# Attention and gated MLP in one kernel: 12 transposes per head, seven PSUM banks for the last batch, and an order written by the kernel's own list scheduler

## The chip, the cores and the metric

The kernel runs on one core of a Trainium2 chip. The time is the device time of one execution in microseconds (us). Of the kernel before there are three runs: 828.46, 829.50 and 830.23 us, median 829.5 us. The engines are called PE (TensorE), PEld (its weight load), DVE (VectorE), ACT (ScalarE), POOL (GpSimd) and SP (SyncE, which issues all of this kernel's DMAs).

## The reference, cut to what matters

```python
# attention: q, k, v are (8, 8, 576, 64), s is (8, 8, 576)
scores = q @ k.T / 8
cum    = cumsum(max(s, 0))
scores = where(causal, scores + min(-(cum_q - cum_k), 0), -1e9)
attn   = exp(scores - max) ; attn /= sum(attn) + 1e-9
x      = (attn @ v) with the 8 heads of a batch side by side       # (8, 576, 512)
# MLP, for each of the 8 batches
h      = gelu_tanh(x @ w_in)                                        # (576, 1024)
u, v   = h[:, :512], h[:, 512:]
v_n    = layer norm of v over its columns * g_ln
v_s    = w_sg @ v_n + b_sg                                          # over the 576 tokens
out    = x + (u * v_s) @ w_out
```

## The kernel before, in words

There are 64 heads, and after every eighth a batch of the MLP has its input. Heads 0 to 11 run attention in fp32; from head 12 on (scores from head 8) each operand is split in two fp32r parts, high and low, and a product is two or three matmuls into one PSUM bank.

One head, in the code's steps:

- `load(h)` (L102) issues the DMAs of k, q and v; for heads 0 to 7 the row of running sums `cf` follows into `kf` (L109). `split_head(h)` (L272) splits k and q on ACT and POOL and moves the parts with five DMAs (L281 to L285).
- `scores(h)` computes five blocks of queries (`it` 0 to 4, with 64, 128, 128, 128, 128 rows and 64, 192, 320, 448, 576 keys). Each goes from PSUM through DVE (L305, mask and running minimum) into a buffer `p` (`pbuf[h % 2][it]`), and ACT takes the exponential in place (L315).
- `norm` (L318) divides by the row sums, mostly on POOL (L338). Blocks that do not fill 128 rows or columns are copied into spare columns of others at that step: block 0 goes into columns 384 to 447 of block 3.
- `transposes(h)` puts 128x128 pieces of the normed blocks through PE (L377) into four PSUM tiles `pt`, 13 transposes per head; one of them, `tr(t, 0, 4, 512, 64)`, is the last corner of block 4 (keys 512 to 575) and fills only 64 rows. ACT and DVE copy each tile to SBUF (`pa`, `pb`, `pd`).
- `pv(h)` multiplies them with v into `xx` and `x0` (L450, L468 to L472), and ACT and DVE write the result into `xr`.

One batch of the MLP, `ffn(b)`: POOL splits `xr` into `xs` (L90, L93). Then units, each of which fills one PSUM bank: 5 `v` units (matmul `vm`, L510 to L527; the last reads its small operand `xq` by DMA, L520), 8 `u` units (`um`, L574), 8 `s` units (`sm`, L589 to L593) and 8 `o` units (`om`, L608). After `vm` and `um` the bank is held until DVE, ACT and POOL are through with the gelu (L493 to L496, L539 to L548).

PSUM has eight banks: two for `sc`, two for `pt`/`x0`, one for `xx`, three for all MLP units (`ps_m`).

What sets the order: every step is placed at a time in units of heads (`place`, `spread`), and the program is recorded in that order. The tile framework's scheduler then orders the instructions of each engine by its own cost model; the recorded order is its priority. All engines run their own queue strictly in order.

Of the kernel before, what the change touches and what calls it, by code (L numbers as in the profile page):

```python
# [8 lines left out]
F32 = mybir.dt.float32  # L9
# [40 lines left out]
ENG = {'k': 'sg', 'vs': 'sg', 'xs': 'gg', 'ln': 'sg', 'gt': 'sg', 'w': 'gg', 'ws': 'sv', 'n': 'ggggg', 'n0': 'gggsg', 'ws1': 'g'}  # L50
MT = 52.0
F6 = [2.0, 9.4]
F7 = [2.0, 9.4]
F0 = [1.9, 9.6]
POS = dict(load=-1.8, split=-0.18, sc=(0, 0, 0, 0), tr=(0, 0, 0, 0), pv=(0, 0.1, 0.1), wv=(0.1, 6.0),
           wu=(7.0, 10.0), ws=(9.0, 11.0), wo=(11.0, 14.0), f0=2.0, f1=9.6)


@with_exitstack
def tile_attn_gmlp(  # L60
# [11 lines left out]
):  # L72
    nc = tc.nc

    const = ctx.enter_context(tc.tile_pool(name="const", bufs=1))
    att = ctx.enter_context(tc.tile_pool(name="att", bufs=2))
    moe = ctx.enter_context(tc.tile_pool(name="moe", bufs=1))
    ps_sc = ctx.enter_context(tc.tile_pool(name="ps_sc", bufs=2, space=bass.MemoryType.PSUM))
    ps_pt = ctx.enter_context(tc.tile_pool(name="ps_pt", bufs=2, space=bass.MemoryType.PSUM))
    ps_x = ctx.enter_context(tc.tile_pool(name="ps_x", bufs=1, space=bass.MemoryType.PSUM))  # L80
    ps_m = ctx.enter_context(tc.tile_pool(name="ps_m", bufs=3, space=bass.MemoryType.PSUM))

# [14 lines left out]
    first = []  # L97

    def later():
        return tc.issue_after(first[0].ins)  # L100

# [22 lines left out]

    dram = ctx.enter_context(tc.tile_pool(name="dram", bufs=1, space=bass.MemoryType.DRAM))
    cum = dram.tile([2, BH, S], F32, name="cum")
# [191 lines left out]
    def norm(h, its, rs):  # L318
# [52 lines left out]
    def transposes(h):  # L371
# [42 lines left out]
        t = ps_pt.tile([P, 512], F32, name="pt", tag="pt")  # L414
        tr(t, 0, 4, 512, 64)
        tr(t, 64, 3, 384)
        tr(t, 192, 4, 384)
        if h < NP:
            pt["pd"] = (att.tile([P, 320], F32, name="pdh", tag="pdh", bufs=1),)
            nc.vector.tensor_copy(out=pt["pd"][0][0:64, 0:64], in_=t[0:64, 0:64])  # L420
# [11 lines left out]
    def pv(h):  # L432
# [34 lines left out]
        if f32:  # L467
            nc.tensor.matmul(xx[0:rows, 256:320], st(4)[0:REM], pd[0][0:REM, 0:64], start=False, stop=True)  # L468
            nc.tensor.matmul(x0[0:rows, 0:64], st(0), pd[0][:, 64:128], start=True, stop=True)
        else:  # L470
# [13 lines left out]
    def ffn(b):  # L484
        xs = []
        for c in range(NC):
            t = moe.tile([P, 2, S], F32R, name="xs", tag="xs", bufs=4)
# [80 lines left out]
        def u_unit(ch, dt):  # L568
            cs = slice(ch * CH, ch * CH + CH)
            ps = ps_m.tile([P, 512], F32, name="um", tag="m")  # L570
            n = 0
# [10 lines left out]
        def s_unit(ch, dt):  # L582
            cs = slice(ch * CH, ch * CH + CH)
            ds_ = slice(dt * P, (dt + 1) * P)
            ps = ps_m.tile([P, 512], F32, name="sm", tag="m")
            n = 0
# [14 lines left out]
        def o_unit(ch, mt):  # L601
            cs = slice(ch * CH, ch * CH + CH)
            ms = slice(mt * P, (mt + 1) * P)
            ps = ps_m.tile([P, 512], F32, name="om", tag="m")
            n = 0
# [35 lines left out]

    def spread(gen, t0, t1, total):
        done = [0.0]

        def go():
            c = next(gen, None)
            if c is not None:
                done[0] += c
# [68 lines left out]
```

## Time and profile before

| | |
|---|---|
| median of three runs | 829.5 us |
| the profiled execution's own time | 829.98 us |
| its span, first to last instruction | 828.2 us |
| mean granted clock of PE | 0.992 |
| busy: PE, PEld, DVE, ACT, POOL | 794.3, 695.6, 597.6, 577.4, 597.6 us |

The span is 1.8 us shorter than the execution's own time. A busy PE in this profile means that some matmul is under way; matmuls overlap, so the time that one costs is the distance to the start of the next, not its own length.

### The profile page before, as it was taken

The numbers are of one execution on the slowest core, as the hardware profiler recorded it, in microseconds if no ns is written. First come the engines' busy times: TensorE is split into PE (matmuls) and PEld (weight loads), VectorE is DVE, ScalarE is ACT, GpSimd is POOL, SyncE is SP. The second block draws the span as 40 slices with busy tenths as digits, with TensorE's granted clock in tenths as the row PEclk, the third lists the DMA queues.
The fourth block names the chain that finished last, engine by engine and source line by source line (L and its number), as shares of the span: only waits on it lengthen the run. The fifth ranks groups of instructions, "written<-read, shape, count | busy, mean of one in ns | idle before, by whom it ended". The sixth has DMA issues, their size and how long they took to land.

```text
span 828.2 us, 16736 instructions
## 1 busy us (share of the span) xinstructions
PE 794.3 (96%) x5161; PEld 695.6 (84%) x5161; DVE 597.6 (72%) x1806; ACT 577.4 (70%) x1620; POOL 597.6 (72%) x979
## 2 busy tenths in 40 slices
PE   6899999899999999999999999999999999998898
PEld 3455666799989998999989997899989998997798
DVE  5995468975787678966887687965897678963552
ACT  4787778875686678867787677866887678853340
POOL 4987668888677767796778777796778778782541
PEclk9999999999999999999999999999999999999999
DMA  7656553334342453444434443444434443300001
GB/s 218 193 171 183 146 136 87 95 98 115 104 106 71 128 131 86 103 122 127 118 85 105 130 132 73 113 121 109 112 101 112 122 127 87 99 25 30 27 7 58
DMA packets 69804, 89.29 MB, mean 108 GB/s; under 512 B 25954, under 2 KB 42212, under 8 KB 69716
## 3 DMA queue, kind: packets, MB, share of 16 engines
q1 hardware_dynamic: 69716, 88.23, 40.6%
q8 instruction: 41, 0.67, 0.4%
q14 instruction: 47, 0.39, 0.2%
HBM read 42.27 MB, written 9.73 MB: 63 GB/s over the span
## 4 chain that ended last, share of the span: by engine, by line
PE 73%; DVE 13%; DMA 6%; ACT 3%; issue 3%; POOL 2%; SPq 1%; DVEq 0%; POOLq 0%; ACTq 0%
PE om L608 12%; PE sm L589 11%; PE um L574 10%; PE vm L510 9%; PE xx L450 9%; PE pt L377 8%; PE sc L297 4%; PE sc L298 4%; DVE p L305 2%; DMA q<-k 2%; PE sm L593 1%; DMA xq<-xs 1%; PE sm L592 1%; DVE vm L496 1%; DVE wbits L220 1%
## 5 line engine op out<-in xcount | busy, mean ns | idle before, releaser
L338 POOL TENSOR_SCALAR p<-p,rs 128x448 f32<-128x448 f32 (+4 forms) x372 | 181.0, 500 | 30.5 <-DVE rs L321 10.9
L315 ACT ACTIVATE p<-p,mn 128x448 f32<-128x448 f32 (+4 forms) x320 | 177.9, 557 | 25.5 <-DVE mn L305 23.4
L305 DVE CUSTOM_DVE_ANT_0 p<-sc,mask 64x64 f32<-64x64 f32 (+4 forms) x320 | 126.2, 422 | 55.3 <-PE pt L377 29.6
L377 PE MATMUL pt<-ident,p 128*128 128x128 f32 (+1 forms) x832 | 136.6, 278 | 4.6 <-DVE pbl L389 2.6
L574 PE MATMUL um<-xs,wi 128*128 128x288 f32 x768 | 124.1, 303 | 4.0 <-DVE vt L548 2.0
L589 PE MATMUL sm<-ws,vn 128*128 128x288 f32 x768 | 127.1, 300 | 0.4 <-DVE u L496 0.4
L93 POOL TENSOR_TENSOR k<-raw,k 128x576 fp32r<-128x576 f32 x56 | 80.6, 1439 | 63.7 <-ACT k L88 34.1
L608 PE MATMUL om<-gt,wo 128*128 128x288 f32 x768 | 125.6, 299 | 0.0
L574 PEld LDWEIGHTS um<-xs,wi 128*128 128x128 f32 x768 | 110.0, 191 | 10.3 <-DVE u L496 3.2
L377 PEld LDWEIGHTS pt<-ident,p 128*128 128x128 f32 (+1 forms) x832 | 97.0, 138 | 20.6 <-DVE pbl L389 5.4
L608 PEld LDWEIGHTS om<-gt,wo 128*128 128x128 f32 x768 | 110.5, 188 | 2.6 <-DVE ot L612 0.3
L589 PEld LDWEIGHTS sm<-ws,vn 128*128 128x128 f32 x768 | 109.9, 189 | 2.6 <-DVE u L496 1.5
L510 PE MATMUL vm<-wi,xs 128*128 128x512 f32 x384 | 105.5, 407 | 4.4 <-DVE u L496 2.2
L297 PE MATMUL sc<-k,q 128*128 128x448 f32 x336 | 100.7, 308 | 1.4 <-DVE mn L305 0.8
L298 PE MATMUL sc<-k,q 66*128 66x448 f32 x336 | 89.2, 298 | 0.4 <-DMA k<-cum 0.3
L88 ACT CAST pbh<-pt 128x512 fp32r<-128x512 f32 x104 | 49.0, 479 | 58.1 <-PE pt L377 58.0
L510 PEld LDWEIGHTS vm<-wi,xs 128*128 128x128 f32 x384 | 71.6, 194 | 20.8 <-DVE u L496 2.4
L93 POOL TENSOR_TENSOR gt<-u,gt 128x288 fp32r<-128x288 f32 x64 | 50.9, 807 | 44.3 <-ACT gt L88 43.9
L93 DVE TENSOR_TENSOR pbl<-pt,pbh 128x512 fp32r<-128x512 f32 x104 | 56.6, 549 | 16.8 <-ACT pbh L88 16.7
L297 PEld LDWEIGHTS sc<-k,q 128*128 128x128 f32 x336 | 60.6, 180 | 9.1 <-DVE mn L305 3.6
L298 PEld LDWEIGHTS sc<-k,q 66*128 66x128 f32 x336 | 60.7, 181 | 5.9 <-issue 0.8
L88 ACT CAST k<-raw 128x576 fp32r<-128x576 f32 x56 | 37.6, 671 | 38.8 <-PE sc L297 33.3
(142 smaller groups left out, 1703.2 us busy)
## 6 DMA issues: line engine op xcount, KB each, us to landing
q<-k SPq DMA_DIRECT2D x168, 144.0 KB
raw<-in_kq SPq DMA_DIRECT2D x56, 288.0 KB
vr<-in_vp SPq DMA_DIRECT2D x52, 192.0 KB
out_t<-ot SPq DMA_DIRECT2D x64, 144.0 KB
k<-k SPq DMA_DIRECT2D x56, 144.0 KB
wraw<-in_w_in SPq DMA_DIRECT2D x16, 256.0 KB
kf<-in_kq SPq DMA_DIRECT2D x8, 288.0 KB
qf<-in_kq SPq DMA_DIRECT2D x8, 288.0 KB
```

The lines of the kernel that those rows point to most:

```text
L88: nc.scalar.copy(out=hi, in_=src)
L93: eng_lo.tensor_tensor(out=lo, in0=src, in1=hi.bitcast(F32), op=ALU.subtract)
L297: nc.tensor.matmul(o, d["q1"][:, i0:i0 + r], d["k1"][:, j0:j1], start=True, stop=False)
L298: nc.tensor.matmul(o, q2[h % 2][:, i0:i0 + r], d["k2"][0:66, j0:j1], start=False, stop=True)
L305: nc.vector.tensor_tensor_reduce(out=pbuf[h % 2][it][0:r, j0:j1], in0=pst[0:r, c0:c0 + j1 - j0], in1=(mask2 if it in (2, 4) else mask)[0:r ...
L315: nc.scalar.activation(out=p, in_=p, func=AF.Exp, bias=d["mn"][0:r, it:it + 1], scale=-1.0, accum_out=sums[h % 2][0:r, it:it + 1])
L338: e.tensor_scalar(out=po, in0=pi, scalar1=f, scalar2=1.0, op0=ALU.mult, op1=ALU.mult)
L377: nc.tensor.transpose(out=ps[0:n, c:c + P], in_=pb[it][:, jb:jb + n], identity=ident)
L510: nc.tensor.matmul(ps[0:r], xs[c][:, xi, ts_], wi[:, c, wj, fs], start=(n == 0), stop=(n == 11))
L574: nc.tensor.matmul(ps[:, 0:CH], wi[:, c, wj, dt * P:(dt + 1) * P], xs[c][:, xi, cs], start=(n == 0), stop=(n == 11))
L589: nc.tensor.matmul(ps[:, 0:CH], vn[j][:, vi, ds_], ws[:, j, wj, cs], start=(n == 0), stop=False)
L608: nc.tensor.matmul(ps[:, 0:CH], wo[:, c, wj, ms], gt[ch, c][:, gi, :], start=(n == 0), stop=(n == 11))
```

## The change

It has four parts.

1. `norm` writes the last corner of block 4 into columns 448 to 511 of block 3 (rows 0 to 63), as a separate POOL instruction behind a shorter one for the rest of block 4. The transpose of block 3's last 128 columns then carries the corner along, and the 13th transpose is gone. The evacuation of that tile is cut differently: from head 12 on ACT copies 64x64 and 128x256 instead of 64x128 and 128x192, and DVE has three subtractions (64x64, 64x64, 128x192) instead of two; for heads 0 to 11 one DVE copy goes. In instructions: 64 transposes fewer on PE, 64 more on POOL, 40 more on DVE (104 and 52 fewer, 12 fewer).
2. `ffn` takes its PSUM banks for the last batch in turn from three pools, seven banks in all.
3. All calls are recorded in a `Program` first. `graph` finds their dependencies, `cost` gives each a duration by formula, and `plan` is a list scheduler: of the instructions that are ready it takes the one that can start first, at a tie the one with the lowest key (the step's place in heads). `emit` records them in the order of the planned starts and ties each engine to it. A transfer is planned to move 1300 ns after its issue at the earliest, one transfer after another at 280 GB/s, and its reader to start 600 + 1060 + 100 ns later.
4. Two positions: `split` from -0.18 to -0.4, the end of `wv` from 6.0 to 7.5.

```diff
+LATENCY = [[54, 38, 39, 80, 60], [54, 35, 33, 77, 60], [54, 34, 35, 90, 60], [55, 34, 35, 80, 60], [1060] * 5]
+OVERLAP = [0, 93, 75, 25, 0]
+MARGIN = 100.0
+ISSUE = 450.0
...
+    def cost(self, op):
...
+            if name == "transpose":
+                d, load = 110.0, 56.0
...
+            v = (outs or big)[0]
+            d, load = v.dims[0][1] * v.columns() * 4 / 280.0, ISSUE
...
+def plan(cost, pre, first, uses, order, bufs, prio, after, slack=(0, 0, 0, 0, 0), window=48):
...
+            for c in cand:
+                if c[0] <= least + slack[e]:
+                    if best is None or c[0] < best[0]:
+                        best = (c[0], e, c[1], c[2])
+                    break
...
+        elif e == SP:
+
+            moved = max(moved, s + 1300) + d
+            free[e], end = s + load, moved + 600
...
+            elif it == 4:
+                o = [(p[:, 0:512], p[:, 0:512], rs[:, 4:5]),
+                     (pbuf[h % 2][3][0:64, 448:512], p[0:64, 512:S], rs[0:64, 4:5])]
...
-        tr(t, 0, 4, 512, 64)
         tr(t, 64, 3, 384)
         tr(t, 192, 4, 384)
...
-            nc.scalar.copy(out=hi[0:64, 0:128], in_=t[0:64, 0:128])
-            nc.scalar.copy(out=hi[:, 128:320], in_=t[:, 128:320])
-            nc.vector.tensor_tensor(out=hi[64:128, 0:128], in0=t[0:64, 0:128], in1=hi[0:64, 0:128].bitcast(F32),
+            nc.scalar.copy(out=hi[64:128, 0:64], in_=t[64:128, 64:128])
+            nc.scalar.copy(out=hi[:, 64:320], in_=t[:, 64:320])
+            nc.vector.tensor_tensor(out=hi[0:64, 0:64], in0=t[64:128, 64:128], in1=hi[64:128, 0:64].bitcast(F32),
+                                    op=ALU.subtract)
+            nc.vector.tensor_tensor(out=hi[64:128, 64:128], in0=t[0:64, 64:128], in1=hi[0:64, 64:128].bitcast(F32),
                                     op=ALU.subtract)
...
+        rings = cycle([(ps_m, "m"), (ps_sc, "sc"), (ps_m, "m"), (ps_pt, "pt"), (ps_m, "m"), (ps_sc, "sc"), (ps_pt, "pt")]
+                      if b == B - 1 else [(ps_m, "m")])
...
-            ps = ps_m.tile([P, 512], F32, name="vm", tag="m")
+            ps = bank("vm")
...
+    cost, pre, new, uses, order, bufs, after = nc.graph()
+    prio = [(op["key"], n) for n, op in enumerate(nc.ops)]
+    t, start, _, seqs = plan(cost, pre, new, uses, order, bufs, prio, after)
+    nc.emit(tc, new, uses, seqs, start)
```

Three places of the order matter below. All recorded calls have one line in the changed kernel (L283), so the names tell what a row is.

The first instructions of SP, before: `st` is the input of the running sums, with which everything begins; `kf`, `qf`, `vf` are head 0's and then head 1's.

```order
L128 DMA st<-in_s_t 128x320
L107 DMA kf<-in_kq 128x576
L108 DMA qf<-in_kq 128x576
L118 DMA vf<-in_vp 128x6x64
L107 DMA kf<-in_kq 128x576
```

The same place after the change:

```order
L283 DMA kf<-in_kq 128x576
L283 DMA qf<-in_kq 128x576
L283 DMA vf<-in_vp 128x6x64
L283 DMA st<-in_s_t 128x320
L283 DMA kf<-in_kq 128x576
```

`st` went from first to fourth: head 1's `load` has the key 1 - 1.8 = -0.8, and the start of the program has 0.

PE at the first heads, before, from the first transposes of head 0 on (`p_3_151` is block 3 of head 0, `sc` from `kf` are the scores of head 2):

```order
L377 MATMUL pt<-ident,p_1_148 128x128
L377 MATMUL pt<-ident,p_3_151 128x128 x2
L377 MATMUL pt<-ident,p_4_153 128x128
L295 MATMUL sc<-kf,qf 128x448
L295 MATMUL sc<-kf,qf 64x64
L295 MATMUL sc<-kf,qf 128x320
L295 MATMUL sc<-kf,qf 128x192
L377 MATMUL pt<-ident,p_2_149 128x128
```

After the change, from the end of head 1's product with v on:

```order
L283 MATMUL xx<-pbl,vf 64x448
L283 MATMUL xx<-pbl,vf 64x320
L283 MATMUL xx<-pdh,vf 64x192
L283 MATMUL xx<-pdh,vf 64x64
L283 MATMUL x_377<-pdh,vf 64x64
L283 MATMUL sc<-kf,qf 128x448
L283 MATMUL sc<-kf,qf 64x64
L283 MATMUL sc<-kf,qf 128x320
L283 MATMUL sc<-kf,qf 128x192
L283 MATMUL vm<-wi,xs 128x512
```

The scores of head 2 no longer stand between the transposes of head 0 but behind all work of heads 0 and 1.

PE at the end of the last head, before (`xx` and `x_10809` are its product with v, `vm` and `um` from `xs` are units of the last batch, `om` of the one before):

```order
L608 MATMUL om<-gt,wo 128x288 x12
L450 MATMUL xx<-pdh,vs 128x192
L472 MATMUL x_10809<-pdh,vs 128x64
L450 MATMUL xx<-pdl,vs 128x192
L450 MATMUL xx<-pdh,vs 128x64
L510 MATMUL vm<-wi,xs 128x512 x2
L574 MATMUL um<-xs,wi 128x288
```

After the change (four units of `sm` stand where one and the dots are):

```order
L283 MATMUL xx<-pdh,vs 128x64
L283 MATMUL om<-gt,wo 128x288 x9
L283 MATMUL sm<-ws,vn 128x288 x12
L283 MATMUL sm<-wr_878,vnr_10640 128x288
L283 MATMUL sm<-wr_892,vnr_109 128x288
...
L283 MATMUL om<-gt,wo 128x288 x24
L283 MATMUL vm<-wi,xs 128x512 x6
L283 MATMUL om<-gt,wo 128x288 x12
L283 MATMUL vm<-wi,xs 128x512 x6
```

Between the last matmul of the last head and the first that reads its `xs` there were none; now there are 101 of 288 columns (9 + 56 + 24 + 12) and nine of 512.

## Rows read from the trace of the kernel before

**Rows 1.** The page, parts 1 and 4: busy time, and the chain that ended last.

```profile
PE 794.3 (96%) x5161; PEld 695.6 (84%) x5161; DVE 597.6 (72%) x1806; ACT 577.4 (70%) x1620; POOL 597.6 (72%) x979
PE 73%; DVE 13%; DMA 6%; ACT 3%; issue 3%; POOL 2%; SPq 1%; DVEq 0%; POOLq 0%; ACTq 0%
```

**Rows 2.** Windows: stretch, busy us of PE, PEld, DVE, ACT, POOL; clock, DMA share, GB/s.

```profile
3.00:6.00 3.00, 0.10 (x1) 0.14 (x1) 2.46 (x6) 0.00 (x0) 1.46 (x3) 1.00 0.97 279
...
24.00:41.00 17.00, 15.45 (x62) 7.68 (x60) 15.21 (x43) 12.39 (x37) 15.81 (x25) 0.91 0.58 182
...
60.00:180.00 120.00, 114.47 (x638) 80.81 (x638) 84.50 (x278) 93.69 (x270) 92.24 (x150) 1.00 0.51 130
180.00:740.00 560.00, 553.37 (x3847) 515.80 (x3846) 426.76 (x1305) 419.21 (x1180) 430.48 (x705) 1.00 0.42 106
...
760.80:764.20 3.40, 3.37 (x9) 2.46 (x10) 0.48 (x1) 0.90 (x2) 1.41 (x1) 0.50 0.12 43
```

**Rows 3.** Timeline of PE at the end: start, us, line, count [idle before, releaser].

```profile
756.51 1.74 PE L608 MATMUL om<-gt,wo 128*128 128x288 f32 x12
...
758.40 0.21 PE L450 MATMUL xx<-pdh,vs 128*128 128x64 f32 x1
760.77 1.22 PE L510 MATMUL vm<-wi,xs 128*128 128x512 f32 x2 [2.15 <-POOL xs L90]
...
769.69 2.96 PE L510 MATMUL vm<-wi,xs 128*128 128x512 f32 x12
...
778.06 4.50 PE L510 MATMUL vm<-wi,xs 128*128 128x512 f32 x12 [2.21 <-DVE u L496]
...
787.99 3.19 PE L574 MATMUL um<-xs,wi 128*128 128x288 f32 x12 [2.01 <-DVE vt L548]
```

**Rows 4.** Timeline of all engines behind the last head.

```profile
760.80 1.41 POOL L93 TENSOR_TENSOR xs<-xr,xs 128x576 fp32r<-128x576 f32 x1
```

**Rows 5.** Groups by line and form: busy us, mean ns of one, idle before.

```profile
L377 PE MATMUL pt<-ident,p 128*64 128x128 f32 x64 | 17.6, 276 | 2.1 <-DVE pbl L389 1.8 <-DVE pbl L93 0.3
...
L338 POOL TENSOR_SCALAR p<-p,rs 128x576 f32<-128x576 f32 x64 | 49.1, 767 | 0.0
...
L338 POOL TENSOR_SCALAR p<-p,rs 64x64 f32<-64x64 f32 x128 | 44.2, 346 | 6.1
...
L427 DVE TENSOR_TENSOR pdh<-pt,pdh 64x128 fp32r<-64x128 f32 x52 | 14.8, 284 | 4.4 <-ACT pdh L426 3.0
```

**Rows 6.** Timeline of PE at the first heads.

```profile
25.07 3.15 PE L295 MATMUL sc<-kf,qf 128*128 128x448 f32 x8
...
46.74 0.86 PE L377 MATMUL pt<-ident,p 128*128 128x128 f32 x6
```

**Rows 7.** Timeline of SP at the start.

```profile
0.79 0.39 SPq L128 DMA_DIRECT2D st<-in_s_t  x1
1.23 0.42 SPq L107 DMA_DIRECT2D kf<-in_kq  x1
...
2.89 0.63 SPq L107 DMA_DIRECT2D kf<-in_kq  x1
```

**Rows 8.** Timeline of DVE at the start.

```profile
3.37 0.48 DVE L200 MEMSET vnr<- 2x512 f32 x1
3.89 0.81 DVE L134 TENSOR_SCALAR st<-st 128x320 f32<-128x320 f32 x1
```

**Rows 9.** Waits of PE from 180 to 740 us: total, times, longest.

```profile
PE vm L524 <- DMA xq<-xs: 2.0, 2, 1.4
...
PE sm L593 <- DMA vnr<-vnr: 0.9, 2, 0.4
```

**Rows 10.** The chain around 500 us: start, us from issue to reader.

```profile
502.88 3.65 DMA q<-k
...
507.11 3.36 DMA xq<-xs
```

More of the change, by code (lines that the diff above doesn't have):

```diff
@@ L1 @@
[L1 to L2 removed]
+from bisect import bisect_left, insort
+from contextlib import ExitStack, contextmanager
+from itertools import count, cycle
 import concourse.bass as bass
@@ new lines, with __init__, step, __getitem__ @@
+class View:
+    def __init__(self, buf, dims, off, dt, how):
+        self.buf, self.dims, self.off, self.dtype, self.how = buf, dims, off, dt, how
+    def step(self, dims, off, how, dt=None):
+        return View(self.buf, dims, off, dt or self.dtype, self.how + [how])
+    def __getitem__(self, key):
+        ks = key if isinstance(key, tuple) else (key,)
+        dims, off = [], list(self.off)
+        for n, (s, c) in enumerate(self.dims):
+            k = ks[n] if n < len(ks) else slice(None)
+            a, b = (k, k + 1) if isinstance(k, int) else (k.start or 0, c if k.stop is None else k.stop)
+            off[n == 0] += a * (1 if n == 0 else s)
+            if n == 0 or not isinstance(k, int):
+                dims.append((s, b - a))
+        return self.step(dims, off, lambda x: x[key])
+    def rearrange(self, text, **kw):
+        dims = self.dims
+        if "(" in text:
+            n = 1
+            for _, c in dims[1:]:
+                n *= c
+            dims = [dims[0], (dims[-1][0], n)]
+        return self.step(dims, self.off, lambda x: x.rearrange(text, **kw))
+    def bitcast(self, dt):
+        return self.step(self.dims, self.off, lambda x: x.bitcast(dt), dt)
+    def columns(self):
+        n = 1
+        for _, c in self.dims[1:]:
+            n *= c
+        return n
+    def span(self):
+        lo = self.off[0]
+        return (self.off[1], self.off[1] + self.dims[0][1], lo,
+                lo + 1 + sum(s * (c - 1) for s, c in self.dims[1:]))
+    def make(self):
+        x = self.buf.make()
+        for f in self.how:
+            x = f(x)
+        return x
@@ new lines, in plan, with put, grant @@
+def plan(cost, pre, first, uses, order, bufs, prio, after, slack=(0, 0, 0, 0, 0), window=48):
+    n = len(cost)
+    left = [len(p) for p in pre]
+    succ = [[] for _ in range(n)]
+    for i, p in enumerate(pre):
+        for q in p:
+            succ[q].append(i)
+    issue = [[] for _ in range(n)]
+    for i, qs in after.items():
+        for q in qs:
+            issue[q].append(i)
+            left[i] += 1
+    owner, remain = {}, {}
+    for i in range(n):
+        for b in first[i]:
+            owner[b] = i
+            left[i] += 1
+        for b in uses[i]:
+            remain[b] = remain.get(b, 0) + 1
+    ready = [[] for _ in range(5)]
+    at = [0.0] * n
+    tagof = {b: t for t, bs in order.items() for b in bs}
+    free_slots = {t: [0.0] * bufs[t] for t in order}
+    nxt = {t: 0 for t in order}
+    last = {}
+    def put(j):
+        left[j] -= 1
+        if left[j] == 0:
+            insort(ready[cost[j][0]], (prio[j], j))
+    def grant(t):
+        while free_slots[t] and nxt[t] < len(order[t]):
+            b = order[t][nxt[t]]
+            nxt[t] += 1
+            f = free_slots[t]
+            x = min(f)
+            f.remove(x)
+            j = owner[b]
+            at[j] = max(at[j], x)
+            put(j)
+    for i in range(n):
+        if left[i] == 0:
+            insort(ready[cost[i][0]], (prio[i], i))
+    for t in order:
+        grant(t)
+    free = [0.0] * 5
+    start, fin = [0.0] * n, [0.0] * n
+    pest = peocc = moved = 0.0
+    held = asked = (0.0, 0.0)
+    seqs = [[] for _ in range(5)]
+    for _ in range(n):
+        best = None
+        for e in range(5):
+            cand, least = [], 1e18
+            for pr, i in ready[e][:window]:
+                if e == PE:
+                    s = max(pest + peocc, max(at[i], pest) + cost[i][2])
+                    soon = pest + peocc + 1
+                else:
+                    s = max(at[i], free[e])
+                    soon = free[e]
+                cand.append((s, pr, i))
+                least = min(least, s)
+                if s <= soon:
+                    break
[3 more added lines that the diff above has]
+                        best = (c[0], e, c[1], c[2])
+                    break
+        if best is None:
+            return None
+        s, e, pr, i = best
+        del ready[e][bisect_left(ready[e], (pr, i))]
+        _, d, load, wide, lock = cost[i]
+        if e == PE:
+            pest, peocc, end = s, d, s + d + 60
+            free[e] = s
+        elif e == SP:
+            moved = max(moved, s + 1300) + d
+            free[e], end = s + load, moved + 600
+        else:
+            if e == DVE and wide and held[0] <= s < held[1]:
+                s = held[1]
+            if e == POOL and lock and asked[0] <= s < asked[1]:
+                s = asked[1]
+            end = s + d
+            if wide:
+                asked = (s, end)
+            if lock:
+                held = (s, end)
+            free[e] = end - OVERLAP[e]
+        start[i], fin[i] = s, end
+        seqs[e].append(i)
+        for j in issue[i]:
+            at[j] = max(at[j], s)
+            put(j)
+        for j in succ[i]:
+            ej = cost[j][0]
+            at[j] = max(at[j], s if e == ej == PE else end + LATENCY[e][ej] + MARGIN)
+            put(j)
+        for b in uses[i]:
+            remain[b] -= 1
+            last[b] = max(last.get(b, 0.0), end)
+            if remain[b] == 0:
+                free_slots[tagof[b]].append(last[b] + 60)
+                grant(tagof[b])
+    return max(fin), start, fin, seqs
```

212 lines of the change are left out of this document (187 added, 25 removed).

## The prediction

> **What bounds the kernel now.** I read the page's busy times first, then the chain, then the windows by stage, and only then the timeline where the windows show PE idle. PE is busy in 96% of the span, and its lines hold 73% of the chain that ended last; DVE, ACT and POOL are busy for 70 to 72% each [rows 1]. The windows say where that holds. From 180 to 740 us PE is idle for 6.6 of 560 us, so that there a microsecond of PE work is a microsecond of the time. From 60 to 180 us it is idle for 5.5 us and from 24 to 41 us for 1.55 us [rows 2]: these are the fp32 heads, where softmax and the weights' conversion keep PE waiting. The third place is the end. Behind the last head's product, which starts its last matmul at 758.40 us, PE waits three times: 2.15 us for POOL's `xs`, 2.21 us for a DVE instruction of a `u` unit and 2.01 us for one of a `v` unit [rows 3]. The last two are no data of the waiting matmul: `vm` at 778.06 us and `um` at 787.99 us start a new accumulation, and what they need is one of the three banks that the gelu still holds. After the first of these idle stretches the granted clock is 0.50 for 3.4 us, that is 1.2 instead of 2.4 GHz [rows 2], and the starts after the other two are as slow: 12 `vm` take 4.50 us there against 2.96 us at 769.69 us, and 12 `um` 3.19 us against 1.74 us for 12 `om` of the same size [rows 3].
>
> The sum is made against the profiled execution's 829.98 us (span 828.2 us and 1.8 us around it). The median of the three runs stands 0.5 us lower, so I take 0.5 us off at the end.
>
> **The 13th transpose.** 64 matmuls and their weight loads go. One is 276 ns long [rows 5], but transposes overlap: six of them take 0.86 us, of which the last is 0.28 us, so each costs (0.86 - 0.28) / 5 = 0.116 us, about 0.11 us with the shorter operand [rows 6]. 64 x 0.11 = 7.0 us. From 180 us on, with 44 of the heads, PE is the bound and this counts in full; of the first 20 heads' 2.2 us some may turn into waiting. Ends: 4.8 us, and 17.7 us if a transpose cost its whole length. I take -7.0 us.
>
> **What it costs elsewhere.** POOL has one instruction more per head. The 128x576 division (767 ns) loses an eighth of its columns and a 64x64 one (346 ns) is added [rows 5]; block 3's last transpose must now wait for both. 64 x 346 ns = 22.1 us of POOL at most, on an engine that is idle 28% of the span [rows 1]; PE's other work of the same heads and batches hides it. DVE gets one instruction of at most 284 ns more for 52 heads, 14.8 us in all [rows 5], ACT nothing to speak of. I take both at nothing; uncovered, POOL's would cost up to 22.1 us, which is a rival below.
>
> **The end of the program.** The 2.15 us behind the last head come from a chain through ACT, DVE and POOL that ends with the low part of `xs` at 760.80 + 1.41 = 762.2 us [rows 4], 3.6 us after the last matmul has ended (758.40 + 0.21) [rows 3]. Before, nothing of PE's queue stands in that gap. After, 101 matmuls of 288 columns and nine of 512 stand between the last matmul of the last head and the first that reads its `xs`. At 1.74 / 12 = 0.145 us and 2.96 / 12 = 0.25 us [rows 3] that is 16.9 us, over four times the chain: this wait goes. The two bank waits go because a unit takes one of seven banks: with three, a unit waits for the gelu three units back, 5 to 8 us of PE work; with seven, for that seven back, 12 us or more. With the waits goes the slow clock behind them. The stall is 2.15 + 2.21 + 2.01 = 6.4 us; the slow starts cost 4.50 - 2.96 = 1.5 us, 3.19 - 1.74 = 1.4 us, and 3.4 us at half clock = 1.7 us [rows 2, 3], 4.7 us in all. Of these 11.1 us I take 9.1, since one new wait of 2 us (DVE or POOL, whose units now come closer together) is what such a tail has shown three times. Ends: 0 and 11.1 us.
>
> **The start.** The load of `st` is issued fourth instead of first, behind three transfers of 768 KB. Its issue moves from 0.79 us to about where the fifth DMA's stood less one slot, that is by 2.89 - 1.23 = 1.66 us [rows 7]. DVE takes `st` at 3.89 us, right behind a memset that ends at 3.85 us [rows 8]; how long it had lain there no row shows, so the delay is 0 at least. At most the transfers ahead must be through first: 786 kB at 279 GB/s [rows 2] is 2.8 us. I take the shift of the issue, +1.7 us, since PE's first matmul and all of the weights' loads hang on `st`. The Trainium skill (DMA: Bandwidth & Descriptors, "Issuing engines are not separate DMA queues") says that all DMAs run on the same 16 engines and interleave there; by that the delay is not the issue alone but part of the transfers too, towards the 2.8 us. Its table of measured rates gives 341 GB/s for 1 MB, by which the upper end would be 2.3 us, an estimate; the row's 279 GB/s is the one that is used.
>
> Then the scores of head 2: before, they fill 3.15 us of PE between the transposes of head 0 [rows 6]. After, they come behind head 1, so that this filler is missing once and head 2's softmax is late. Ends: 0, where they wait for their own load anyway, and 3.15 us plus as much again for the softmax behind it. I take +1.0 us.
>
> **The middle.** Everything else stands in another order as well, and the trace can't show an order that did not run. Waits of PE for transfers are 2.0 us (`xq`) and 0.9 us (`vnr`) [rows 9]. The plan charges a transfer 1300 + 600 + 1060 + 100 ns plus its bytes, 3.3 to 3.6 us for these sizes; the chain shows 3.36 us for `xq` and 3.65 us for a part of q [rows 10]. An order planned with that puts other work into the time, so I take -2.0 us of the 2.9. Ends: the whole idle time of PE, 6.6 + 5.5 + 1.55 = 13.6 us, goes, or as much comes.
>
> Sum: 829.98 - 7.0 - 9.1 + 1.7 + 1.0 - 2.0 = 814.6 us; less 0.5, **814.1 us**.
>
> **The rivals.**
>
> *POOL becomes the wait of every head (slower).* The last transposes of a head wait for block 4's corner, which is now the last of seven POOL instructions. The list scheduler puts a waiting instruction on PE just when its input should be ready, with 100 ns to spare; PE's queue is in order, so `pt`, and behind it the scores, `xx` and MLP units, wait if POOL is late. Price: the added 346 ns in each of 64 heads, 22.1 us [rows 5], 836.2 us. It decides from (829.5 - 814.1) / 64 = 0.24 us per head. For it: nothing in the trace has less room than 100 ns. Against it: POOL idles 28% [rows 1], and PE's list of waits over the middle has the transfers at its head, no `p` of POOL [rows 9]. The Trainium skill would add a second road to it (SBUF — State Buffer, "Who interferes with whom": GpSimd and VectorE hold a shared port exclusively); no row here prices it.
>
> *The end stays as it is.* The seven banks and the longer queue only move the waits: a `v` unit's chain through DVE, ACT and POOL is as long as before, and the `s` units need it. Then only transposes, start and middle count: 814.1 + 9.1 = 823.2 us. For it: all three waits end in DVE or POOL [rows 3]. Against it: the waiting matmuls needed a bank or the first `xs`, not the unit's result.
>
> *The order clears the middle too.* All 13.6 us of idle time go instead of 2.0: 814.1 - 11.6 = 802.5 us. For it: the waits are short and scattered, and MLP units that could fill them lie ready. Against it: in the fp32 heads PE waits for DVE and POOL, which have the same work as before [rows 2].
>
> **How the numbers follow.** Forecast 50 in 100, end stays 19, middle cleared 18, POOL late 13. The likeliest one's own range is 808 to 820 us: the transposes' ends and the start's. The whole range reaches to the end that stays with some new waits, 828, and to the middle nearly cleared, 803; it leaves out POOL's 13 and some 6 of the middle's. 0.2% is 1.7 us, about what a measurement of this kernel can tell from no change: the bounds are 827.8 and 831.2 us. Faster: forecast 50, middle 18, end 16 of 19 = 84. Slower: 12 of POOL's 13. Within: 4.
>
> **What the profile after would show.** Right: 768 `pt` on PE, and its interval from 180 us on shorter by 0.11 us a head; no PE wait of 2 us after the last head, and a clock of 1.00 there; DVE takes `st` later by 1 to 3 us. Wrong: PE waits for POOL `p` or ACT `pd` in each head; idle stretches between 24 and 180 us well over 7 us; a wait of the `s` units for `vn` in the last 60 us.

## The result, and the profile after

The changed kernel takes 836.9 us (median of five runs, 834.4 to 839.2), the kernel before 829.5 us beside it (827.9 to 830.2). The ratio is 1.0091, 95% interval [1.0066, 1.0116]: slower by 7.4 us by the medians, where 814.1 us was forecast and 828 us at most. Below, "percent" always means against the kernel before on the same chip.

The page of the changed kernel, parts 1 and 4, answers to [rows 1]:

```profile
span 835.4 us, 16823 instructions
...
PE 795.3 (95%) x5097; PEld 688.4 (82%) x5097; DVE 607.0 (73%) x1846; ACT 581.9 (70%) x1620; POOL 607.3 (73%) x1043
...
PE 75%; DVE 7%; ACT 6%; POOL 6%; DMA 2%; issue 2%; SPq 0%; POOLq 0%; DVEq 0%; ACTq 0%
```

64 matmuls are gone, and PE's busy time has not fallen. Its windows (stretch; busy us of PE, PEld, DVE, ACT, POOL; clock, DMA share, GB/s) answer to [rows 2]:

```profile
60.00:180.00 120.00, 107.28 (x586) 76.27 (x587) 90.76 (x276) 92.28 (x266) 92.28 (x157) 0.99 0.47 121
180.00:740.00 560.00, 549.72 (x3698) 499.29 (x3697) 430.67 (x1337) 419.89 (x1170) 431.82 (x743) 1.00 0.43 110
740.00:835.00 95.00, 91.34 (x636) 87.01 (x636) 50.29 (x120) 35.91 (x86) 43.43 (x77) 1.00 0.10 31
```

From 180 to 740 us PE is idle for 10.3 us instead of 6.6, but it starts 149 matmuls fewer there, of which 45 are transposes that the edit takes out: a matmul that waits in the pipeline counts as busy. So I counted starts. For each matmul I took the time to the next one's start, less the median of that time for its kind in both kernels. The medians add up to PE's work; what is over is lost:

| us | first matmul | work | lost 0–41 | 41–180 | 180–740 | 740–end | percent |
|---|---|---|---|---|---|---|---|
| before | 5.90 | 767.0 | 9.0 | 14.0 | 15.8 | 12.9 | |
| after | 8.52 | 760.0 | 5.5 | 21.4 | 34.5 | 1.9 | +0.91 |
| order_13tr | 8.91 | 767.0 | 6.0 | 16.2 | 29.8 | 1.1 | +0.50 |
| order_all_later | 8.21 | 760.0 | 2.4 | 18.8 | 33.6 | 0.3 | +0.41 |
| kept_12tr | 5.89 | 760.0 | 9.8 | 21.4 | 22.1 | 11.1 | +0.75 |
| kept_no_13th | 5.90 | 760.0 | 9.5 | 15.8 | 19.7 | 12.9 | -0.19 |
| kept_pool_split | 5.89 | 767.0 | 10.1 | 19.3 | 14.6 | 12.9 | +0.66 |
| kept_then_planned | 5.89 | 767.0 | 9.6 | 13.4 | 21.4 | 0.6 | -0.77 |

(Each row but the percent is of one profiled execution. How finely kinds are told apart moves the level of a column by several us, the differences between rows by about 1 us. Two executions differ too: kept_7banks, below, has the order of before on every engine up to the last batch, and up to there its matmuls start at most 1.9 us away from those of before. The profiled execution of order_all_later was 2.8 us faster than that run's median, the one of kept_no_13th 2.9 us slower.) The work fell by 7.0 us as forecast, the end gained 11.0 us, and the middle, 41 to 740 us, lost 26.1 us.

The end on PE (start, us, line, count) answers to [rows 3]. The last matmul of the last head starts at 759.94 us, four `s` units and two `o` units come first, and `vm` waits for nothing:

```profile
759.94 0.22 PE L283 MATMUL xx<-pdh,vs 128*128 128x64 f32 x1
...
761.25 1.75 PE L283 MATMUL sm<-ws,vn 128*128 128x288 f32 x12
...
771.82 1.56 PE L283 MATMUL vm<-wi,xs 128*128 128x512 f32 x6
773.23 1.75 PE L283 MATMUL om<-gt,wo 128*128 128x288 f32 x12
774.81 1.57 PE L283 MATMUL vm<-wi,xs 128*128 128x512 f32 x6
```

The start, SP and DVE, answers to [rows 7, 8]. `st` is issued at 2.41 us instead of 0.79, DVE takes it at 7.00 us instead of 3.89:

```profile
2.41 0.63 SPq L283 DMA_DIRECT2D st<-in_s_t  x1
```

```profile
7.00 0.33 DVE L283 TENSOR_SCALAR st<-st 128x320 f32<-128x320 f32 x1 [3.14 <-DMA st<-in_s_t]
```

In the middle, the waits of PE and of its weight loads from 180 to 740 us (total, times, longest), which answer to [rows 9], now have POOL at their head:

```profile
PE pt L283 <- POOL p L283: 2.5, 6, 0.8
...
PE sm L283 <- DMA vnr<-vnr: 0.4, 1, 0.4
```

```profile
PEld pt L283 <- POOL p L283: 7.4, 23, 1.1
```

### The profile page after: what moved, and what is told of

Same layout as the page of the kernel before. It is cut to its first block, busy times and chain, and to the rows that moved or that the text cites. A ratio compares the mean times of both kernels' runs of the same rounds, so it can differ in the third digit from the quotient of the medians.

```text
span 835.4 us, 16823 instructions
## 1 busy us (share of the span) xinstructions
PE 795.3 (95%) x5097; PEld 688.4 (82%) x5097; DVE 607.0 (73%) x1846; ACT 581.9 (70%) x1620; POOL 607.3 (73%) x1043
## 4 chain that ended last, share of the span: by engine, by line
PE 75%; DVE 7%; ACT 6%; POOL 6%; DMA 2%; issue 2%; SPq 0%; POOLq 0%; DVEq 0%; ACTq 0%
PE sm L283 13%; PE om L283 12%; PE xx L283 11%; PE sc L283 10%; PE vm L283 10%; PE pt L283 9%; PE um L283 9%; POOL p L283 3%; ACT p L283 2%; DVE p L283 1%; DMA raw<-in_kq 1%; DVE vt L283 1%; DVE u L283 1%; PE x L283 1%; ACT xr L283 1%
## 5 line engine op out<-in xcount | busy, mean ns | idle before, releaser
L283 POOL TENSOR_SCALAR p<-p,rs 128x512 f32<-128x512 f32 (+3 forms) x436 | 194.5, 457 | 37.7 <-DVE rs L283 22.5
L283 ACT ACTIVATE p<-p,mn 128x448 f32<-128x448 f32 (+4 forms) x320 | 177.8, 557 | 37.2 <-DVE mn L283 35.7
L283 PE MATMUL pt<-ident,p 128*128 128x128 f32 x768 | 154.4, 283 | 10.5 <-POOL p L283 5.0
L283 DVE CUSTOM_DVE_ANT_0 p<-sc,mask 128x448 f32<-128x448 f32 (+4 forms) x320 | 124.6, 419 | 32.8 <-PE sc L283 23.8
L283 PE MATMUL sc<-k,q 66*128 66x288 f32 (+9 forms) x672 | 142.2, 313 | 4.0 <-DVE mn L283 2.0
L283 PE MATMUL um<-xs,wi 128*128 128x288 f32 x768 | 135.6, 305 | 3.1 <-DVE vt L283 2.3
L283 PE MATMUL sm<-ws,vn 128*128 128x288 f32 x768 | 135.5, 305 | 1.2 <-DVE u L283 1.0
L283 PE MATMUL om<-gt,wo 128*128 128x288 f32 x768 | 132.4, 301 | 0.0
L283 PEld LDWEIGHTS pt<-ident,p 128*128 128x128 f32 x768 | 95.5, 141 | 39.7 <-POOL p L283 12.2
L283 PE MATMUL vm<-wi,xs 128*128 128x512 f32 (+1 forms) x416 | 124.6, 407 | 0.0
L283 PEld LDWEIGHTS um<-xs,wi 128*128 128x128 f32 x768 | 113.0, 190 | 7.0 <-DVE vt L283 4.1
L283 PEld LDWEIGHTS sm<-ws,vn 128*128 128x128 f32 x768 | 112.9, 190 | 4.3 <-DVE u L283 3.5
L283 PEld LDWEIGHTS sc<-k,q 128*128 128x128 f32 (+3 forms) x672 | 102.3, 183 | 16.1 <-DVE mn L283 4.5
L283 PEld LDWEIGHTS om<-gt,wo 128*128 128x128 f32 x768 | 112.3, 189 | 2.1 <-POOL gt L283 0.2
L283 POOL TENSOR_TENSOR k<-raw,k 128x576 fp32r<-128x576 f32 x56 | 80.2, 1432 | 36.2 <-ACT k L283 36.2
L283 PEld LDWEIGHTS vm<-wi,xs 128*128 128x128 f32 (+1 forms) x416 | 72.8, 185 | 11.4 <-POOL xs L283 0.2
L283 POOL TENSOR_TENSOR gt<-u,gt 128x288 fp32r<-128x288 f32 x64 | 50.6, 805 | 32.3 <-ACT gt L283 32.1
L283 POOL TENSOR_TENSOR vs<-vr,vs 128x384 fp32r<-128x384 f32 x52 | 52.6, 1011 | 27.5 <-ACT vs L283 26.0
L283 DVE SCALAR_TENSOR_TENSOR u<-u,um 128x288 f32<-128x288 f32 x128 | 56.4, 443 | 14.3 <-ACT u L283 13.4
L283 DVE TENSOR_TENSOR pbl<-pt,pbh 128x512 fp32r<-128x512 f32 x104 | 56.6, 549 | 8.8 <-ACT pbh L283 8.4
L283 ACT CAST pbh<-pt 128x512 fp32r<-128x512 f32 x104 | 49.5, 481 | 17.1 <-PE pt L283 16.8
L283 ACT ACTIVATION_READ_ACCUMULATOR p<-p,mn 128x1 f32 (+1 forms) x320 | 60.4, 189 | 0.0
```

Of the source, the lines that this page charges most:

```text
L283: r = getattr(op["eng"].real, op["name"])(*[f(a) for a in op["args"]], **{k: f(v) for k, v in op["kw"].items()})
```

## The experiments

**Is it the order or the transposes?** order_13tr is the changed kernel with the old `norm`, `transposes` and `pv`. old_12tr is the kernel before with the new ones, arranged by its own scheduler; old_12tr_7banks has `bank` too.

```
-            elif it == 4:                               # order_13tr; old_12tr: +
-                o = [(p[:, 0:512], ...), (pbuf[h % 2][3][0:64, 448:512], p[0:64, 512:S], ...)]
+        tr(t, 0, 4, 512, 64)                            # order_13tr; old_12tr: -
```

> The changed kernel with the 13 transposes and the undivided 576-column division of before; list order and banks as changed. Theory A (the list-planned order puts block 4's and the other blocks' transposes just behind POOL, whatever the corner does): PE still loses 12 to 16 us at `pt` between 180 and 740 us, and the 64 extra transposes cost about 7.0 us: 844 us. Theory B (the added POOL instruction makes POOL late in every head): the waits for POOL go, so 836.9 + 7.0 - 16 to 22: 822 to 828 us.

> The kernel before with the 12 transposes alone (the corner in block 3); order and banks as before. Theory A: nothing waits, the transposes' 7.0 us come back: 822.5 us, `pt` without a wait for POOL from 180 us on. Theory B: POOL is late in each head, up to 346 ns x 64 = 22.1 us against 7.0 us: 829.5 to 844.6 us.

> The kernel before with 12 transposes and the seven banks of the last batch; order as before. Theory A: 822.5 us less the two bank waits and the slow starts behind them (2.21 + 2.01 + 1.5 + 1.4 = 7.1 us), while the 2.15 us for `xs` stay: about 815.4 us. Theory B: 823 to 838 us. If the banks only move the waits at the end: 822.5 us.

Measured: 834.3 us, +0.50% [0.32, 0.69]; 841.2 us, +1.38% [1.10, 1.65]; 840.9 us, +1.44% [1.19, 1.70]. order_13tr lies between its two theories: without the 12 transposes the planned order is 0.4% faster than with them (the intervals touch), where theory A had it 7 us slower and B 9 to 15 us faster. In the old kernel they cost 11 us: A's gain of 7 us fell there, B's range holds for the first and is passed by 3 us in the second. But the old kernel's scheduler had rearranged everything too. One thing A had right: order_13tr, without the added instruction, waits for `p` as well, so that this wait of the changed kernel comes with the planned order (PE, 180 to 740 us):

```profile
PE pt L283 <- POOL p L283: 4.1, 5, 1.0
```

**The edits in the order of before.** From here on "kept" kernels are built through the new `emit`, with a table of places instead of `plan`; the table holds the order in which the kernel before stands, and an added instruction goes right behind the one that it was split from. The way of building costs nothing by itself: kept_7banks is before's program up to the last batch, and over the first 180 us its matmuls start within 0.7 us of before's.

```
-    t, start, _, seqs = plan(cost, pre, new, uses, order, bufs, prio, after)
+    start = list(accumulate(array("h", decompress(b85decode(ORDER_TABLE)))))
+    seqs = [sorted((i for i in range(len(start)) if cost[i][0] == e), key=start.__getitem__) for e in range(5)]
```

> The kernel before with every instruction of every engine kept in its order (the order is written out as a table), and the 12 transposes put into it: 64 transposes go, each corner division stands right behind block 4's, the added DVE instruction right behind the one it was split from. Three banks, `st` first. Theory E (the new arrangement, not the work, costs the time; any edit lets the scheduler shuffle everything): the 7.0 us of the transposes come back, 821.5 us with 828.5 for before. Theory W (the added work on POOL, DVE and ACT costs it in any order): 829 to 841 us, as in the run with 12 transposes alone in the scheduler's own order.

> The kernel before with every instruction in its order and its 13 transposes; only the last batch's units take their bank in turn from seven instead of three. If the two bank waits and the slow starts behind them go: 828.5 - 7.1 = 821.4 us. If the chain through DVE and ACT at the end sets the time, banks or not: 828.5 us within 1.5 us.

> Both edits in the kept order of before. Theory E: 828.5 - 7.0 - 7.1 = 814.4 us, the time that was predicted. Theory W: 822 to 834 us.

Measured: 833.7 us, +0.75% [0.47, 1.03]; 826.8 us, -0.16% [-0.37, 0.06]; 833.3 us, +0.66% [0.42, 0.90]. With nothing else moved, the 12 transposes cost about 6 us where 7 were forecast as a gain. And the banks alone give little. Their PE timeline at the end shows why:

```profile
771.72 3.36 PE L348 MATMUL um<-xs,wi 128*128 128x288 f32 x24
774.92 2.94 PE L348 MATMUL vm<-wi,xs 128*128 128x512 f32 x12
...
786.27 0.53 PE L348 MATMUL sm<-ws,vn 128*128 128x288 f32 x2 [2.21 <-ACT vn L348]
788.43 0.55 PE L348 MATMUL sm<-ws,vn 128*128 128x288 f32 x1 [1.62 <-POOL vn L348]
788.77 4.78 PE L348 MATMUL um<-xs,wi 128*128 128x288 f32 x24
```

The two bank waits of [rows 3] are gone, PE is up to 8.5 us earlier than before, and then the `s` units wait for `vn` and the starts after it are slow (24 `um` in 4.78 us, against 3.36 us at 771.72 us).

**One part at a time.** kept_no_13th leaves out the 64 matmuls only, and what read their columns reads others of the same bank; kept_pool_split and kept_dve_split keep them and split one instruction on POOL or DVE; kept_12tr_late makes the whole edit from head 18 on.

```
-        tr(t, 0, 4, 512, 64)                                             # kept_no_13th
+            elif it == 4:                                                # kept_pool_split
+                o = [(p[:, 0:512], p[:, 0:512], rs[:, 4:5]), (p[0:64, 512:S], p[0:64, 512:S], rs[0:64, 4:5])]
-            nc.vector.tensor_tensor(out=hi[64:128, 0:128], ...)          # kept_dve_split: 0:64 and 64:128
+            elif it == 4 and h >= 18:                                    # kept_12tr_late
```

> The kernel before with every instruction in its order, only the 13th transposes (64 matmuls) left out and nothing added on any engine: what read their columns reads other columns of the same bank, so the corner's values are not the reference's. This is the term of -7.0 us by itself. Theory F (PE is the bound, its work comes off the time): 828.3 - 7.0 = 821.3 us. Theory G (PE's saved time turns into waiting for chains of DVE, POOL, ACT and transfers that don't get shorter): -2 to -4 us, 824 to 826 us.

> The kernel before with every instruction in its order and its 13 transposes; POOL divides block 4 in two instructions (128x512 and, in place, 64x64) instead of one of 128x576: POOL's added instruction alone, about 0.25 us a head. If POOL's part makes the hidden cost of 12.3 us: 834 to 840 us. If POOL's idle 28% cover it: 828.3 us within 1.5 us.

> The kernel before with every instruction in its order and its 13 transposes; DVE's subtraction of 64x128 columns in the 52 fp32r heads is made in two of 64x64: DVE's added instruction alone, 0.14 to 0.25 us a head. If DVE's part makes the hidden cost, since `x0` waits for `pdh` and the scores for `mn`: 831 to 838 us. If it is covered: 828.3 us within 1.5 us.

> The kernel before with every instruction in its order; heads 0 to 17 keep 13 transposes, heads 18 to 63 have 12 (with all that comes with them on POOL, DVE and ACT). Theory S (the added work costs in the stretch up to 170 us, where POOL, DVE and ACT are busy for 98 to 100% of 10 us at a time in before): the 5 us lost there don't come, 827 to 829 us, no loss and little gain. Theory H (it costs the same in every head): 5.3 to 6.2 us x 46 / 64 = 3.8 to 4.5 us, 832 us.

Measured: 826.3 us, -0.19% [-0.37, -0.01]; 833.7 us, +0.66% [0.46, 0.87]; 831.1 us, +0.35% [0.21, 0.49]; 826.6 us, -0.15% [-0.33, 0.03]. In us of 828: -1.6, +5.5 and +2.9, together +6.8; the whole edit measured +6.2. Each of these figures is uncertain by 1 to 2 us, so the close fit is in part luck. kept_dve_split has no change of the first partition (last section), and ACT's new cut was not run alone. Theories G and S hold to within 0.5 us, and H falls: heads 0 to 17 carry all of the loss.

Where the 7.0 us go: PE comes earlier and waits. One such place is at 345 us of kept_no_13th (SP, then PE), where the transfer of `vnr` stands behind one of `cum` in SP's queue and does not move up:

```profile
345.01 0.26 SPq L347 DMA_DIRECT2D k<-cum  x1
345.36 0.47 SPq L347 DMA_DIRECT2D vnr<-vnr  x1
```

```profile
349.41 0.94 PE L347 MATMUL sm<-wr,vnr 66*128 66x288 f32 x5 [1.82 <-DMA vnr<-vnr]
```

In the kernel before the same transfer and the same matmul:

```profile
345.47 0.47 SPq L561 DMA_DIRECT2D vnr<-vnr  x1
```

```profile
348.14 0.30 PE L593 MATMUL sm<-wr,vnr 66*128 66x288 f32 x1
```

PE was 0.7 us ahead of before when it got there, and 1.3 us behind it afterwards.

Where POOL costs: not in each head. Matching every matmul of kept_pool_split with its own start in before, PE is 1.0 us late up to 140 us, 6.7 us from 160 us on, and 5.1 us at the end. The windows of before in that stretch, and of kept_pool_split:

```profile
140.00:150.00 10.00, 9.49 (x68) 8.78 (x67) 9.51 (x28) 9.78 (x31) 9.83 (x15) 1.00 0.44 110
150.00:160.00 10.00, 8.72 (x57) 7.30 (x57) 10.00 (x29) 7.40 (x22) 8.13 (x13) 1.00 0.43 109
160.00:170.00 10.00, 9.12 (x67) 8.45 (x65) 8.45 (x25) 7.95 (x23) 9.72 (x18) 1.00 0.45 110
```

```profile
140.00:150.00 10.00, 9.38 (x68) 8.53 (x65) 9.09 (x25) 9.80 (x30) 10.00 (x14) 1.00 0.42 111
150.00:160.00 10.00, 7.99 (x51) 6.58 (x52) 9.94 (x29) 8.03 (x22) 6.95 (x13) 1.00 0.46 109
160.00:170.00 10.00, 7.74 (x51) 6.85 (x51) 8.99 (x20) 5.26 (x17) 7.66 (x14) 0.93 0.32 82
170.00:180.00 10.00, 9.54 (x52) 8.52 (x50) 6.17 (x21) 6.15 (x18) 5.18 (x12) 0.73 0.15 42
```

Here the last weights are converted beside the first fp32r heads, and POOL, DVE and ACT are full in turn: 9.83, 10.00 and 9.78 of 10 us. PE's waits there (140 to 180 us) are for DVE's `mn`, 1.8 us, and `pdh`, 0.9 us, not for POOL. How POOL makes DVE late, the rows of the weights' conversion `wbits` show, in before, then in kept_pool_split with the POOL instructions beside it:

```profile
160.37 0.45 DVE L220 SCALAR_TENSOR_TENSOR wbits<-wraw,wbits 128x256 int32<-128x256 int32 x1
161.44 1.29 DVE L222 SCALAR_TENSOR_TENSOR wbits<-wraw,wbits 128x256 int32<-128x256 int32 x1
```

```profile
162.33 2.42 DVE L348 SCALAR_TENSOR_TENSOR wbits<-wraw,wbits 128x256 int32<-128x256 int32 x1
165.37 1.86 DVE L348 SCALAR_TENSOR_TENSOR wbits<-wraw,wbits 128x256 int32<-128x256 int32 x1
```

```profile
163.19 1.27 POOL L348 TENSOR_TENSOR vn<-vt,vn 128x512 fp32r<-128x512 f32 x1
165.55 1.40 POOL L348 TENSOR_TENSOR k<-raw,k 128x576 fp32r<-128x576 f32 x1
```

The conversion has all its operands in SBUF. The same instruction takes 0.41 us where nothing of POOL runs beside it (155.63 us in before); beside POOL's `vn` or `k` it lasts until 0.3 us after their end. DVE's `u<-u,um`, with `um` in PSUM, takes 0.40 to 0.46 us all 128 times, beside POOL or not. So part of DVE's full 10 us is time in which it is held. The added POOL instruction shifts the two queues against each other, and this pair takes 4.28 us instead of 1.74; in kept_12tr_late, which has no loss, it takes 1.73. PE, kept waiting, then runs at a granted clock of 0.50 from 169 to 175 us, the lower of its two levels:

```profile
164.95 1.87 PE L589 MATMUL sm<-ws,vn 128*128 128x288 f32 x12 [0.36 <-DVE u L496]
```

```profile
169.45 3.25 PE L348 MATMUL sm<-ws,vn 128*128 128x288 f32 x12 [0.80 <-DVE u L348]
```

These are the same matmuls in before and in kept_pool_split. PE is 2.0 us late ahead of the pair and 6.7 us behind it. That POOL holds DVE there is read from these rows; no run took the conversion away.

**Why the planned order loses in the middle.** order_pool_later plans PE's reads of POOL 400 ns later, order_all_later those of ACT and DVE too; order_corner_act puts the corner's division on ACT; order_break_costs tells the planner what follows a change of the first partition (last section). All are planned anew.

```
-LATENCY = [..., [54, 35, 33, 77, 60], [54, 34, 35, 90, 60], [55, 34, 35, 80, 60], [1060] * 5]
+LATENCY = [..., [454, 35, 33, 77, 60], [454, 34, 35, 90, 60], [455, 34, 35, 80, 60], [1060] * 5]   # order_pool_later: 455 alone
...
+        if base != rows[e]:                             # order_break_costs
+            rows[e] = base
+            s = max(s, free[e] + BREAK[e])              # BREAK = [0, 112, 105, 117, 0]
...
-                if e is nc.scalar:                      # order_corner_act
+                if e is nc.scalar or (it == 4 and n == 1):
```

> The changed kernel with one number of its planner changed: a PE instruction that reads what POOL wrote is planned 455 instead of 55 ns behind it. Theory A: the losses at `pt` between 180 and 740 us fall from 16 us to under 6 us, other work stands ahead of the transposes, and the time is 10 us or more shorter: 820 to 828 us. Theory B (POOL has too much work): the same waits, 836.9 us within 2 us.

> The changed kernel with three numbers of its planner changed: a PE instruction that reads what ACT, DVE or POOL wrote is planned 400 ns later than the planner has it. With POOL alone it was 0.4% faster than the changed kernel. Theory A (PE's queue is planned with too little room for the others): less is lost between 180 and 740 us than the changed kernel's 34.3 us, 25 us or less, and the time is 826 to 831 us. Theory P (any order of this planner loses about 30 us there, whatever the room): 832 to 838 us.

> The changed kernel with the corner's division (64x64, 346 ns) of every head on ACT instead of POOL, planned so. Theory B (POOL's added instruction makes every head late): most of what the 12 transposes cost comes back, 9.6 us less: about 827 us. Theory C: POOL's chain of a head is 0.3 us shorter and ACT's 0.2 us longer, 3 to 6 us faster: 831 to 834 us. Theory D: another order of the same kind, 834 to 838 us.

> The changed kernel whose planner is told what the trace shows at a change of the operands' first partition: the next instruction starts 112 (ACT), 105 (DVE) or 117 ns (POOL) later. Work and transposes as changed. Theory C1 (PE waits since the plan doesn't know these breaks and puts transposes too early): of the 16 us that PE loses at `pt` between 180 and 740 us, 10 go: 825 to 829 us. Theory C2 (the breaks cost by themselves, whether they are planned or not): `pt` loses less, other work as much more: 834 to 838 us.

Measured: 833.1 us, +0.49% [0.33, 0.65]; 831.6 us, +0.41% [0.23, 0.59]; 839.5 us, +1.35% [1.20, 1.50]; 841.0 us, +1.55% [1.40, 1.71]. More room ahead of PE's reads is worth 0.4 to 0.5%, but the loss from 180 to 740 us stays at 34 to 38 us in all four (34.5 in the changed kernel), and what the planner knew better about the chip, or less work on POOL, came out slower, by more than any theory on record had. What the room gained came earlier: in order_pool_later about 5 us less are lost from 41 to 180 us. Theory P stands, as a description of the loss: six orders of this planner lose 30 to 38 us there (order_all_later's time lies 0.4 us under P's range). Which of its choices does it is open. One change in the order shows everywhere: PE goes from one kind of work to another 1381 times from 180 to 740 us, before 1092 times. That this costs the time was not tried, and old_12tr speaks against it: with 1039 changes it loses 13 us more there than before.

**Single changes in the changed kernel's own order.**

```
-            nc.scalar.copy(out=hi[64:128, 0:64], in_=t[64:128, 64:128])     # order_full_copy
+            nc.scalar.copy(out=hi[:, 0:64], in_=t[:, 64:128])
...
+    seqs[SP].remove(i); seqs[SP].insert(0, i); start[i] = -1.0              # order_st_first, i: the load of st
```

> The changed kernel, the same order of every instruction; only ACT's copy of the corner (`pdh` 64x64 at partition 64, 52 heads) is made over all 128 partitions and the same 64 columns. In the changed kernel's trace an ACT instruction that begins on another partition than the one before it starts about 20 ns after that one's end, one on the same partition about 97 ns before it; so 104 such changes cost ACT 104 x 0.115 = 12 us. Theory C (these breaks make the chain behind the transposes late): ACT's busy queue is shorter by 12 us and a part of it reaches PE: 2 to 8 us faster, 829 to 835 us. Theory D (the order alone loses the time, PE waits for POOL, not for ACT): 836.9 us within 1.5 us.

> The changed kernel, the same order of every instruction but one: the load of `st` is issued first again, ahead of the three loads that stood ahead of it. PE's first matmul was 2.6 us later in the changed kernel (8.52 against 5.90 us). If all hangs on it: 836.9 - 2.6 = 834.3 us. If the first scores of head 0 wait for the other loads instead, which now come 0.45 us later: no change.

Measured: 832.8 us, +0.61% [0.48, 0.74]; 834.6 us, +0.67% [0.49, 0.84]. The first is 0.3% faster than the changed kernel, the second 0.24%, its first matmul at 5.55 us; the intervals still touch those of the changed kernel. In the kept order the full copy gave nothing:

> The same with ACT's copy of the corner made over all 128 partitions, so that no ACT instruction there changes its first partition (2.9 us in the changed kernel's order). If the breaks cost in any order: 2 to 4 us less than the run without it. If they only cost where an order leaves no room: the same within 1 us.

834.9 us, +0.78% [0.47, 1.10], against +0.66% [0.42, 0.90] without it.

**The better half of each.** kept_then_planned takes the first 7,096 instructions, up to what PE starts at 620 us in before, from the table, and leaves the rest to `plan`; 13 transposes, seven banks.

```
+        if k < len(kept):
+            i = kept[k]
+            e = cost[i][0]
...
```

> The kernel before with its 13 transposes and its order kept for all that PE starts before 620 us; behind that the planner orders the rest, and the last batch has seven banks. It joins what each order did well: the middle of before (15.8 us lost from 180 to 740 us against 34.3) and the end of the changed kernel (1.8 us lost behind 740 us against 12.9). Expected: 828.3 - 9 to 11 = 817 to 819 us. If the planner's order loses in the last 120 us of heads as it does from 180 us on (0.03 us per us): 821 to 823 us. If the gain at the end came from what stood in the middle: no gain, 828 us.

Measured: 822.4 us, -0.77% [-1.01, -0.54], faster than both kernels. The end is the changed kernel's: PE is busy for 78.05 us, 0.6 us lost, at full clock:

```profile
740.00:822.00 82.00, 78.05 (x543) 74.50 (x541) 38.69 (x82) 24.53 (x53) 35.35 (x62) 1.00 0.11 34
```

It loses 5.6 us more than before from 180 to 740 us (21.4 against 15.8): 3.3 us behind 620 us, where the second theory's 0.03 us per us allowed for 3.6, and 2.3 us in the part that has the order of before.

## Why the prediction was wrong

*The 13th transpose, -7.0.* PE's work fell by just that, 767.0 to 760.0 us. The step that failed is the next: "PE is the bound and this counts in full". Alone it was worth 1.6 us (0.1 to 3.1 by the interval). PE at 553 of 560 us [rows 2] says that PE is rarely idle, not that it is never held: once it is ahead, transfers and DVE chains hold it.

*What it costs elsewhere, nothing.* This step failed too. In the kept order POOL's and DVE's instructions measured +5.5 and +2.9 us. I took 28% idle over the span [rows 1] as cover; the stretch of 140 to 170 us has none, and I read it only inside a window of 120 us in which DVE is busy for 70% [rows 2]. A price for POOL's hold on DVE, of which the prediction says that no row gives one, stood in before's trace: `wbits` takes 0.41 us alone and 1.29 us beside POOL. In the planned order the edit costs 9.9 us of waits (55.9 against 46.0 us lost from 41 to 740 us) for 7.0 us of work.

*The end, -9.1.* Measured -11.0 us, the upper bound, and for the reason given first: MLP work of the batch before stands between the last head and the first `xs`. But the banks, to which I gave the larger part, are worth 0.16% by themselves: the rival "the end stays" was right on them, and it took the planned order as well. What that order gives at the end with three banks was not run.

*The start, +1.7 and +1.0.* The first matmul came 2.6 us later, near the upper bound, and `st` 3.1 us later, over it, though its issue moved by 1.6 us only: the transfers ahead count. That agrees with the Trainium skill (DMA: Bandwidth & Descriptors, "Issuing engines are not separate DMA queues"), by which DMAs run on the same 16 engines and interleave there; the prediction's estimate of 2.3 us from its table of rates was too low. The loss of scores as filler did not come: up to 41 us 3.5 us less is lost. Net -0.9 instead of +2.7.

*The middle, -2.0.* Measured +26.1 us, nearly twice the bound of 13.6 us, which I had taken from PE's idle time and which counts no waiting matmul. About 16 us of it are the planned order's (46.0 us lost from 41 to 740 us in order_13tr, 29.8 us in before), 10 us the transposes'. This is the term that turned the sign. The step behind the -2.0 us held by itself: PE's waits for transfers fell from 2.9 us [rows 9] to 0.4 us. What failed is that nothing was charged for the new order's other waits, for POOL and DVE above all, and that idle time was taken as the bound on them. Why this planner's order loses so much is open.

*The rival "POOL becomes the wait of every head"* gave 836.2 us, and 836.9 came. Its number was right by luck and its mechanism half: PE waits for `p` now, but so it does in order_13tr, without the added instruction, and for that instruction no price of 346 ns in each head was found. In the kept order it is paid before head 18, where POOL holds DVE; in the planned order the whole edit costs 5.2 us up to 180 us and 4.7 us behind. That the planner leaves 100 ns is a part at most, since 400 ns more gained 0.4% and left the loss from 180 to 740 us.

## What to carry over

Work added on an engine that idles 28% is not free: look for the 10 us in which it is full, ask which other engine its instructions hold up there, and price the edit there; and work taken off the bound engine is worth only what its next transfer or chain leaves. When an edit is judged through a scheduler, hold the order fixed and change one thing, or the shuffle (from +0.4 to +1.6% among the eight kernels here that a scheduler ordered throughout) hides it. Measure a full engine by the starts of its instructions, not by its busy time, which also grows when an instruction is held.

## What the hardware showed

In the changed kernel's trace an instruction on ACT, DVE or POOL whose data lay ready starts before the one ahead of it has ended, but not where its operands begin on another partition, 64 instead of 0 or the reverse: ACT 97 ns before that end (562 pairs), after a change from partition 64 to 0 12 ns behind it (78 pairs); DVE 76 ns before (459), 31 behind (24), and 13 to 14 behind between the corner's two subtractions (42 pairs); POOL 24 ns before (235), 93 behind (56 and 58). So a change costs 90 to 117 ns, and the corner, which moves between partitions 0 and 64, brings two more on ACT, one more on DVE. ACT's timeline in the changed kernel, and the same place in order_full_copy:

```profile
309.64 0.59 ACT L283 COPY xr<-xx 64x512 f32<-64x512 f32 x1
310.25 0.59 ACT L283 CAST pdh<-pt 64x64 fp32r<-64x64 f32 x2
310.74 0.64 ACT L283 ACTIVATE vt<-vt 128x512 f32<-128x512 f32 x1
```

```profile
308.45 0.59 ACT L283 COPY xr<-xx 64x512 f32<-64x512 f32 x1
309.06 0.49 ACT L283 CAST pdh<-pt 128x64 fp32r<-128x64 f32 x2
309.43 0.65 ACT L283 ACTIVATE vt<-vt 128x512 f32<-128x512 f32 x1
```

From the first to the last start of the two lines on `pdh` and `vt` it is 0.49 us with the change and 0.37 us without. The Trainium skill (VectorE: DVE Perf Modes, "Two Vector instructions with no wait between them") has this for VectorE: an instruction whose operand starts in another group of 32 partitions than the last one there waits until all earlier ones have finished. DVE's 13 to 31 ns behind the end agree with it; that ACT and POOL do the same between partitions 0 and 64 is what these runs add.
